# Weight decode in a one-core attention and MLP kernel: a ScalarE byte read for the low word's bits, and a PSUM bank for the scaled word

## The chip, the cores and the metric

The kernel runs on one core of a Trainium2 chip. The metric is device time in microseconds (us). The core's engines are TensorE (PE, its weight loads PEld), VectorE (DVE), ScalarE (ACT), GpSimd (POOL) and SyncE (SP, which issues the DMAs). Each runs its own instructions strictly in the order of its queue.

## The reference, cut to what matters

```
attn = chunked_attention(q, k, v, mem_k, mem_v)     # 4 x 8 heads x 768 x 64, chunks of 32, window 16+32+8 and 8 memory keys
x  = attn as (3072, 512)
h  = x @ w_in                                        # 512 -> 2048
g  = (a0 + a1 h + a2 h^2 + a3 h^3) / (1 + |b0||h| + |b1| h^2 + 1e-6)
x  = g @ w_out                                       # 2048 -> 512
y  = ((x @ w1) * (x @ w2)) @ w3 @ w_out              # 512 -> 1024, gated, 1024 -> 1024 -> 512
```

The second MLP's matrices are called w1, w2 (together w12), w3 and w_out2 in the kernel. The MLP weights arrive as 64-bit floats; the kernel itself turns each word into a 32-bit float and splits that into two fp32r parts, a high one and a remainder. Every matrix product is made of three TensorE products (high x high, high x low, low x high).

## The kernel before

The 3072 tokens are eight blocks of 384. For every block six attention units (`attend`) fill `xr`, then sixteen steps of the first MLP follow: `gemm1` (12 matmuls into a bank of the PSUM ring `h`), the rational function on ScalarE, GpSimd and VectorE, and four steps later `gemm2` (12 matmuls into the banks acc0 to acc3). After 128 such steps the second MLP runs: `gemm3` (two times 12 matmuls into `h`, called `ab` in the trace), a gate, and `gemm4`; w3 and w_out2 are first multiplied with each other (`w3o`), row block by row block.

Weights come in 72 chunks of 128x512 words, each handled by `decode`: 32 for the first block's steps (w_in, w_out), and 40 for the second MLP (16 of w12, 8 of w_out2, 16 of w3), most of which lie within the last sixteen steps of the first MLP and the time after. A chunk takes a slot of the ring `raw` (4 slots, SBUF) and then:

- `load` (L210): a DMA of 512 KB, issued by SP once the slot's last reader is done.
- `scale` (L214, ScalarE): the word's upper half, read as a float, times 2^-112, in place.
- `low` (L218, VectorE): the lower half shifted right by 29, in place.
- two `join`s (L222, VectorE): upper half shifted left by 3 or'ed with those bits, then the sign bit or'ed in. Both inputs and the output lie in SBUF.
- `high_part` (L226, ScalarE) and `low_part` (L229, GpSimd) write the two parts into wA, wB or w3's tiles; then the slot is free.

The order of all work is the result of a planner, `order`: each piece is a `step` with a nominal time `t`, a cost per engine, the steps it comes after and the rings that it takes a buffer of. The planner's list is written out in that order, so every engine's queue is fixed before the run. The PSUM banks are rings too: `h` has three, `att` one (used by the attention units of all blocks but the first for scores, transposes and outputs in turn), acc0 to acc3 one each. `w3o` takes `acc3` and `att` by turns.

Of the kernel before, what the change touches and what calls it, by code (L numbers as in the profile page):

```python
# [26 lines left out]
NF1 = F1 // P  # L27
# [7 lines left out]
SIGN = -2 ** 31  # L35
# [3 lines left out]
def attention_rational_mlp_gated_mlp(  # L39
# [15 lines left out]
    pe, act, dve, pool, sp = nc.tensor, nc.scalar, nc.vector, nc.gpsimd, nc.sync  # L55
# [11 lines left out]
    wB = const.tile([P, NF1, 2, DM], F32R, name="wB")  # L67
# [6 lines left out]
    att = ExitStack()  # L74
# [7 lines left out]
    def bank(tag, name):  # L82
        return ps.tile([P, DM], F32, tag=tag, bufs=rings[tag], name=name)
# [111 lines left out]
    def raw(name):  # L195
        return rawp.tile([P, DM, 2], I32, tag="raw", name=name)

# [3 lines left out]

    def decode(t, src, dst, *ready, take=(), early=(), LOW=None):

        r, d = [], []

        def load():
            r.append(raw("w64"))
            sp.dma_start(out=r[0], in_=src.bitcast(I32).rearrange("p (k t) -> p k t", t=2))  # L210

        def scale():
            hi = r[0][:, :, 1].bitcast(F32)
            act.activation(out=hi, in_=hi, func=AF.Copy, scale=2.0 ** -112)  # L214

        def low():
            lo = r[0][:, :, 0]
            dve.tensor_scalar(out=lo, in0=lo, scalar1=29, scalar2=None, op0=ALU.logical_shift_right)  # L218

        def join(op, n):  # L220
            lo, hi = r[0][:, :, 0], r[0][:, :, 1]
            dve.scalar_tensor_tensor(out=lo, in0=hi, scalar=n, in1=lo, op0=op, op1=ALU.bitwise_or)  # L222

        def high_part():
            d.append(dst() if callable(dst) else dst)
            act.activation(out=d[0][:, 0], in_=r[0][:, :, 0].bitcast(F32), func=AF.Copy)  # L226

        def low_part(eng):
            eng.tensor_tensor(out=d[0][:, 1], in0=r[0][:, :, 0].bitcast(F32), in1=d[0][:, 0].bitcast(F32),  # L229
                              op=ALU.subtract)  # L230

        a = step(t, {"dma": 1.46}, load, *early, take=("raw",))
        b = step(t, {"act": 0.58}, scale, a)
        c = step(t, {"dve": 0.335}, low, a, port=True)
        c = step(t, {"dve": 0.602}, lambda: join(ALU.logical_shift_left, 3), b, c, port=True)
        c = step(t, {"dve": 0.602}, lambda: join(ALU.bitwise_and, SIGN), c, port=True)
        h = step(t + H0, {"act": 0.58}, high_part, c, *ready, take=take)
        l = step(t + H0, LOW or LOWA, low_part, h, frees=[a], port=True)
        a.until.append(h)
        return h, l  # L240

    def mm3(out_, w, wi, x, xi, first, last):
# [112 lines left out]
    def rat_inv(n, i):  # L355
# [3 lines left out]
        else:  # L359
            act.activation(out=h, in_=Q, func=AF.Exp, scale=-1.0)  # L360

# [134 lines left out]
    PAIR7 = two('d', .551, .27); LOWB = two('p', 1.225, .602); GLO7 = two('p', .956, .469); GATE = two('p', .956, .469)  # L496
    LOWA, PAIR, GLO, XLO = two('p', 1.225, .602), two('p', .551, .27), two('p', .956, .469), two('d', 1.764, .87)
    H0 = 1.098
    FIN = {"act": 0.48, "dve": 0.6}

    def start():
# [71 lines left out]

    for u in range(UPB):
        attend(u)
    for t, o, f in chunks:
        (WO if o else WI)[f] = decode(t, *((w_out[f], wB[:, f]) if o else (w_in[f], wA_slot(f))))
    u = UPB
    for n in range(n1):
        ffn1(n)  # L580
# [10 lines left out]
    sec = step(n1 - 16, {"none": 0.0}, second, *VL.values(), v_[NU - 1], tc_[NU - 1])  # L591
# [9 lines left out]
    DW, D3, DV = -2.122, -5.330, -1.521  # L601
    W12, WO2, W3, OP, G3, G4, X2 = {}, {}, {}, {}, {}, {}, {}
    for f in range(NF1):
        W12[f] = decode(tG[f // 2] + f % 2 * 0.4 + DW, w12[f], wA_slot(f), G1[n1 - NF1 + f], early=[G1[n1 - NF1 + max(0, f - 1)]], LOW={"dve": .602} if f < 0 else LOWB)
    for j in range(NF2):
        WO2[j] = decode(tO[0] + DV + 0.3 * j, w_out2[j], wB[:, j], G2[n1 - NF1 + j], early=[G2[n1 - NF1 + j]], LOW=LOWB)

    def x2(blk):
        t = tG[blk * NF2]
# [43 lines left out]
        gates[m] = ffn2_in(m)  # L653
    O = {}
    for i in range(NF2):
        W3[i] = [decode(tO[i] + 0.5 * g + D3, w3T[i, :, g], w3_dst(i, g), sec, take=("w3",), early=[sec] if i < 2 else [O[i - 2]], LOW=LOWB) for g in range(2)]
        t = tO[i]
        tag = ("acc3", "att")[i % 2]
        o = O[i] = step(t, {"pe": 5.61}, lambda i=i: w3o(i), *[x for p in W3[i] for x in p], *[x for p in WO2.values() for x in p],
                 G2[n1 - 1], *([G4[i - 2]] if i > 1 else []), take=(tag,), frees=[p[0] for p in W3[i]])  # L660
# [82 lines left out]
```

## Time and profile before

| | |
|---|---|
| median of 3 runs | 1188.74 us (1188.38 to 1191.08) |
| the profiled execution | 1193.64 us, of which span 1191.8 us |
| busy, share of the span | PE 94%, PEld 87%, DVE 56%, ACT 56%, POOL 40% |
| mean granted TensorE clock | 0.983 |

The whole-span shares hide three stages. In the first 180 us or so the weights of the first MLP are decoded beside the first block and PE has gaps; from there to about 655 us PE is never idle; between 655 and 797 us, where the second MLP's weights are decoded, it has gaps again; then it is busy to the end. Busy shares of a stretch, and what the engines wait for in it, say what limits it.

### The profile page before, as it was taken

The numbers are of one execution on the slowest core, as the hardware profiler recorded it, in microseconds if no ns is written. First come the engines' busy times: TensorE is split into PE (matmuls) and PEld (weight loads), VectorE is DVE, ScalarE is ACT, GpSimd is POOL, SyncE is SP. The second block draws the span as 40 slices with busy tenths as digits, with TensorE's granted clock in tenths as the row PEclk, the third lists the DMA queues.
The fourth block names the chain that finished last, engine by engine and source line by source line (L and its number), as shares of the span: only waits on it lengthen the run. The fifth ranks groups of instructions, "written<-read, shape, count | busy, mean of one in ns | idle before, by whom it ended". The sixth has DMA issues, their size and how long they took to land.

```text
span 1191.8 us, 18531 instructions
## 1 busy us (share of the span) xinstructions
PE 1121.2 (94%) x7104; PEld 1042.2 (87%) x7104; DVE 668.2 (56%) x1249; ACT 667.0 (56%) x1267; POOL 476.4 (40%) x444
## 2 busy tenths in 40 slices
PE   5587699999999999999999799989999999999998
PEld 4476589999999999999999699978889999999997
DVE  6799896667776677676767878855301010110100
ACT  4576687777787777777777866543312222222121
POOL 2466665444444444444444556633211111111111
PEclk9988799999999999999999999989999999999999
DMA  8535322121121121211220232643101101011000
GB/s 241 153 89 167 107 89 63 37 69 37 47 63 36 43 66 44 62 37 43 74 95 1 76 123 84 210 137 107 36 27 54 53 1 53 1 53 54 1 27 27
DMA packets 28028, 83.07 MB, mean 70 GB/s; under 512 B 3746, under 2 KB 3874, under 8 KB 27938
## 3 DMA queue, kind: packets, MB, share of 16 engines
q1 hardware_dynamic: 27648, 81.80, 22.1%
q8 instruction: 56, 0.92, 0.3%
q14 instruction: 32, 0.26, 0.1%
q10 hardware_dynamic: 292, 0.09, 0.0%
HBM read 69.30 MB, written 12.58 MB: 69 GB/s over the span
## 4 chain that ended last, share of the span: by engine, by line
PE 76%; DVE 7%; DMA 5%; ACT 5%; POOL 4%; issue 3%; SPq 0%; POOLq 0%; DVEq 0%; ACTq 0%
PE acc L245 28%; PE ab L245 19%; PE h L245 18%; PE w3o L245 4%; PE sc L262 3%; DVE w L222 2%; DMA w<-in_w_dram 2%; PE xo L308 2%; POOL wA L229 2%; DMA w<-in_w_in_dram 2%; DMA w<-in_w_out_dram 2%; PE at L299 1%; DVE w L218 1%; POOL wB L229 1%; ACT A L334 1%
## 5 line engine op out<-in xcount | busy, mean ns | idle before, releaser
L245 PE MATMUL h<-xr,wA 128*128 128x384 f32 x1536 | 308.7, 351 | 27.9 <-DVE A L372 26.7
L245 PEld LDWEIGHTS h<-xr,wA 128*128 128x128 f32 x1536 | 277.6, 195 | 35.6 <-DVE A L372 30.8
L245 PE MATMUL acc<-gh,wB 128*128 128x384 f32 x1024 | 287.4, 343 | 1.5 <-POOL wB L229 1.5
L245 PE MATMUL ab<-xr,wA 128*128 128x384 f32 x1536 | 280.1, 337 | 5.0 <-DVE W L460 4.5
L245 PEld LDWEIGHTS ab<-xr,wA 128*128 128x128 f32 x1536 | 271.2, 189 | 10.8 <-DVE W L460 5.1
L346 POOL TENSOR_TENSOR W<-W,Q 128x384 f32<-128x384 f32 x128 | 132.9, 1038 | 211.1 <-ACT Q L342 172.6
L460 DVE TENSOR_TENSOR W<-W,ab 128x384 f32<-128x384 f32 x64 | 35.4, 553 | 288.7 <-PE ab L245 287.5
L245 PEld LDWEIGHTS acc<-gh,wB 128*128 128x128 f32 x1024 | 186.2, 188 | 7.4 <-POOL wB L229 2.3
L245 PE MATMUL acc<-gl,wB 128*128 128x384 f32 x512 | 171.7, 335 | 0.0
L469 POOL TENSOR_TENSOR gl<-W,gh 128x384 fp32r<-128x384 f32 x56 | 56.8, 1016 | 280.4 <-ACT gh L464 280.4
L381 POOL TENSOR_TENSOR gl<-A,gh 128x384 fp32r<-128x384 f32 x128 | 136.7, 1069 | 41.1 <-ACT gh L376 33.9
L364 DVE SCALAR_TENSOR_TENSOR A<-A,cf,h 128x384 f32<-128x384 f32 x128 | 78.0, 609 | 102.4 <-ACT h L360 101.8
L222 DVE SCALAR_TENSOR_TENSOR w<-w 128x512 int32<-128x512 int32 x144 | 119.7, 854 | 5.9 <-ACT w L214 5.3
L456 ACT COPY W<-ab 128x384 f32<-128x384 f32 x64 | 30.7, 480 | 142.8 <-PE ab L245 142.8
L334 ACT ACTIVATE A<-h,cf 128x384 f32<-128x384 f32 x128 | 85.5, 668 | 43.0 <-PE h L245 42.3
L358 ACT ACTIVATE Q<-W,one 128x384 f32<-128x384 f32 x128 | 78.9, 616 | 41.0 <-POOL W L346 40.5
L245 PEld LDWEIGHTS acc<-gl,wB 128*128 128x128 f32 x512 | 96.4, 188 | 0.0
L464 ACT CAST gh<-W 128x384 fp32r<-128x384 f32 x56 | 28.7, 512 | 117.2 <-DVE W L460 110.7
L342 ACT ACTIVATE Q<-W,cf 128x384 f32<-128x384 f32 x128 | 90.8, 709 | 4.0
L245 PE MATMUL acc<-wB,gh 128*128 128x512 f32 x294 | 92.2, 394 | 0.0
L351 DVE TENSOR_TENSOR A<-A,h 128x384 f32<-128x384 f32 x128 | 70.1, 548 | 15.9 <-ACT W L334 14.2
L353 DVE SCALAR_TENSOR_TENSOR A<-A,cf,h 128x384 f32<-128x384 f32 x128 | 77.7, 607 | 2.3 <-ACT W L334 0.6
(61 smaller groups left out, 1401.4 us busy)
## 6 DMA issues: line engine op xcount, KB each, us to landing
qk<-in_qkT_dram SPq DMA_DIRECT2D x48, 320.0 KB, 3.9
w<-in_w_out_dram SPq DMA_DIRECT2D x24, 512.0 KB, 4.5
v<-in_vW_dram SPq DMA_DIRECT2D x48, 192.0 KB, 2.4
w<-in_w_in_dram SPq DMA_DIRECT2D x16, 512.0 KB, 4.8
w<-in_w3T_dram SPq DMA_DIRECT2D x16, 512.0 KB, 3.8
w<-in_w_dram SPq DMA_DIRECT2D x16, 512.0 KB, 4.5
x2d<-x2o SPq DMA_DIRECT2D x16, 384.0 KB, 2.7
x<-x2d SPq DMA_DIRECT2D x16, 384.0 KB, 4.1
```

What stands on the lines that cost most here:

```text
L222: dve.scalar_tensor_tensor(out=lo, in0=hi, scalar=n, in1=lo, op0=op, op1=ALU.bitwise_or)
L229: eng.tensor_tensor(out=d[0][:, 1], in0=r[0][:, :, 0].bitcast(F32), in1=d[0][:, 0].bitcast(F32), op=ALU.subtract)
L245: pe.matmul(out_, lhsT=wi(w, a), rhs=xi(x, c), start=first and i == 0, stop=last and i == 2)
L334: act.activation(out=t, in_=hps[n][src], func=func, scale=scale, bias=bias)
L342: act.activation(out=t, in_=hps[n]["W"], func=AF.Identity, scale=cf[:, 5:6], bias=cf[:, 4:5])
L346: pool.tensor_tensor(out=W, in0=W, in1=Q, op=ALU.mult)
L351: dve.tensor_tensor(out=A, in0=A, in1=h, op=ALU.mult)
L353: dve.scalar_tensor_tensor(out=A, in0=A, scalar=cf[:, 1:2], in1=h, op0=ALU.add, op1=ALU.mult)
L358: act.activation(out=Q, in_=W, func=AF.Ln, bias=one)
L364: dve.scalar_tensor_tensor(out=A, in0=A, scalar=cf[:, 0:1], in1=r, op0=ALU.add, op1=ALU.mult)
L381: eng.tensor_tensor(out=gl, in0=hps.pop(n)["A"], in1=gt[n].bitcast(F32), op=ALU.subtract)
L469: eng.tensor_tensor(out=gl, in0=hps.pop(m), in1=gt[m].bitcast(F32), op=ALU.subtract)
```

## The change

`decode` gets two options. With `byte`, the lower half's top three bits are no longer shifted out by VectorE: ScalarE reads the lower half's top byte (every eighth byte of the chunk), multiplies it by 1/32, subtracts 0.484375 and writes the rounded integer in the lower half's place. With `tag`, `scale` writes to a PSUM bank of the ring `tag` instead of in place; the first join reads that bank and the lower half and writes the bank, the second reads the upper half (SBUF) and the bank and writes SBUF. `inps`, the form in which the value stays in PSUM, is used by no chunk, since all low parts are GpSimd's.

In the first MLP all 32 chunks take the byte read, and of each three one is untagged, one takes a bank of `h`, one the bank `att` (11, 11 and 10 chunks). In the second MLP every other chunk takes both options, with bank `att` (20 of 40); the others are as before. `w3o` now takes `acc3` alone. One nominal time (R[1], that of the step |h|) moves from 0.64 to 0.92, and the planner's cost of a join is 0.64 where it reads PSUM. In the listings after the change line numbers are larger: `scale` is L220, the byte read L226, the VectorE shift L228, the joins L233 and L235, `high_part` L243, `low_part` L246.

```diff
-    def decode(t, src, dst, *ready, take=(), early=(), LOW=None):
+    def decode(t, src, dst, *ready, take=(), early=(), LOW=None, tag=None, byte=False):
...
         def scale():
             hi = r[0][:, :, 1].bitcast(F32)
-            act.activation(out=hi, in_=hi, func=AF.Copy, scale=2.0 ** -112)
+            b.append(bank(tag, "wx") if tag else hi)
+            act.activation(out=b[0], in_=hi, func=AF.Copy, scale=2.0 ** -112)
-        def low():
+        def low(eng):
             lo = r[0][:, :, 0]
-            dve.tensor_scalar(out=lo, in0=lo, scalar1=29, scalar2=None, op0=ALU.logical_shift_right)
+            if eng is act:
+                top = r[0].bitcast(U8).rearrange("p k (t b) -> p k t b", b=4)[:, :, 0, 3]
+                act.activation(out=lo, in_=top, func=AF.Copy, scale=1.0 / 32, bias=-0.484375)
+            else:
+                dve.tensor_scalar(out=lo, in0=lo, scalar1=29, scalar2=None, op0=ALU.logical_shift_right)
-        def join(op, n):
-            lo, hi = r[0][:, :, 0], r[0][:, :, 1]
-            dve.scalar_tensor_tensor(out=lo, in0=hi, scalar=n, in1=lo, op0=op, op1=ALU.bitwise_or)
+        def join(i):
+            lo, hi, x = r[0][:, :, 0], r[0][:, :, 1], b[0].bitcast(I32)
+            if i == 0:
+                dve.scalar_tensor_tensor(out=x if tag else lo, in0=x, scalar=3, in1=lo, op0=ALU.logical_shift_left, op1=ALU.bitwise_or)
+            else:
+                dve.scalar_tensor_tensor(out=x if inps else lo, in0=hi, scalar=SIGN, in1=x if tag else lo, op0=ALU.bitwise_and,
+                                         op1=ALU.bitwise_or)
...
-        b = step(t, {"act": 0.58}, scale, a)
-        c = step(t, {"dve": 0.335}, low, a, port=True)
-        c = step(t, {"dve": 0.602}, lambda: join(ALU.logical_shift_left, 3), b, c, port=True)
-        c = step(t, {"dve": 0.602}, lambda: join(ALU.bitwise_and, SIGN), c, port=True)
+        s = step(t, {"act": 0.58}, scale, a, take=(tag,) if tag else ())
+        c = step(t, {"act": 0.58} if byte else {"dve": 0.335}, low, a, port=not byte)
+        J = {"dve": 0.64 if tag else 0.602}
+        c = step(t, J, lambda: join(0), s, c, port=not tag)
+        c = step(t, J, lambda: join(1), c, frees=[a] if inps else [s], port=not tag)
...
-        o = w3os[i] = bank(("acc3", "att")[i % 2], "w3o")
+        o = w3os[i] = bank("acc3", "w3o")
...
+    TAGS, BYTE, LOWS = (None, "h", "att"), (True,), (LOWA,)
+    TAGT, BYTT, LOWT = (None, "att"), (False, True), (LOWA,)
...
-    R = (0.00,0.64,0.28,0.40,0.44,0.36,0.64,0.52,0.83,0.81,1.11,1.39,1.21,1.59)
+    R = (0.00,0.92,0.28,0.40,0.44,0.36,0.64,0.52,0.83,0.81,1.11,1.39,1.21,1.59)
```

Three places in the queues. First VectorE near its start, before the change. The names w_110, w_127, w_152 are three chunks' raw slots; L218 is the shift, L222 a join; e, sc and sm belong to the attention.

```order
L222 SCALAR_TENSOR_TENSOR w_110<-w_110 128x512
L218 TENSOR_SCALAR w_127<-w_127 128x512
L218 TENSOR_SCALAR w_152<-w_152 128x512
L273 TENSOR_REDUCE mx<-sc 128x4
L222 SCALAR_TENSOR_TENSOR w_127<-w_127 128x512
L276 TENSOR_TENSOR e_84<-sc,mx 128x384
L222 SCALAR_TENSOR_TENSOR w_127<-w_127 128x512
```

The same place after the change. The shifts are gone from VectorE, and the tagged chunk w_127 is joined through the bank wx.

```order
L235 SCALAR_TENSOR_TENSOR w_110<-w_110 128x512
L233 SCALAR_TENSOR_TENSOR wx<-wx,w_127 128x512
L293 TENSOR_TENSOR e_84<-sc,mx 128x384
L235 SCALAR_TENSOR_TENSOR w_127<-w_127,wx 128x512
L290 TENSOR_REDUCE mx<-sc 128x4
```

Second, ScalarE after the change, at the tenth and eleventh step of the first MLP. L226 is a byte read; L351, L359, L375, L377 and L393 are the rational function's instructions. The chunk w_656, whose byte read stands first here, is one that takes the bank att.

```order
L226 ACTIVATE w_656<-w_656 128x512
L243 ACTIVATE wA<-w_484 128x512
L297 ACTIVATE e_85<-e_85 128x384
L393 CAST gh<-A 128x384
L375 ACTIVATE Q<-W,one 128x384
L377 ACTIVATE h<-Q 128x384
L351 ACTIVATE A<-h,cf 128x384
L351 ACTIVATE W<-h 128x384
L359 ACTIVATE Q<-W,cf 128x384
L226 ACTIVATE w_696<-w_696 128x512
```

And the place 31 rows later in the same queue at which that chunk's scale, which waits for the bank, stands.

```order
L319 COPY aT<-at 96x512
L226 ACTIVATE w_729<-w_729 128x512
L226 ACTIVATE w_866<-w_866 128x512
L220 ACTIVATE wx<-w_656 128x512
L393 CAST gh<-A 128x384
L334 CAST xr<-xo 128x4x64
```

So the byte reads moved into the queue of the rational function, and a tagged chunk can hold its raw slot from its byte read to a scale that is queued far behind it. Third, PE at the products of w3 and w_out2, before the change (w3o are those products, acc gemm4, ab gemm3).

```order
L245 MATMUL ab<-xr,wA 128x384 x24
L245 MATMUL w3o<-wB,w_8521 128x512 x12
L245 MATMUL w3o<-wB,w_8555 128x512 x12
L245 MATMUL acc<-wB 128x512 x9
L245 MATMUL w3o<-wB,w_8582 128x512 x12
L245 MATMUL w3o<-wB,w_8612 128x512 x12
L245 MATMUL acc<-wB 128x512 x9
```

After the change.

```order
L262 MATMUL w3o<-wB,w_8469 128x512 x12
L262 MATMUL w3o<-wB,w_8474 128x512 x12
L262 MATMUL acc<-wB 128x512 x9
L262 MATMUL ab<-xr,wA 128x384 x12
L262 MATMUL w3o<-wB,w_8544 128x512 x12
L262 MATMUL w3o<-wB,w_8550 128x512 x12
L262 MATMUL acc<-wB 128x512 x9
```

Twelve matmuls of gemm3 now stand between gemm4 and the next w3o, which takes the same bank as the w3o before it; the first w3o stands behind 240 matmuls of gemm3 instead of 312.

## Rows read from the trace of the kernel before

**Rows 1.** Windows: length, then busy us (and count) by engine, granted clock, DMA.

```profile
core 0: us, PE busy (x) PEld busy (x) DVE busy (x) ACT busy (x) POOL busy (x), PEclk, DMA share, GB/s
0.00:42.00 42.00, 21.63 (x216) 16.96 (x216) 30.66 (x61) 18.27 (x35) 15.38 (x16) 1.00 0.72 198
42.00:192.00 150.00, 120.11 (x791) 108.75 (x792) 131.12 (x239) 110.40 (x210) 92.50 (x77) 0.90 0.40 122
655.00:727.00 72.00, 59.82 (x324) 57.27 (x324) 61.33 (x97) 55.88 (x107) 42.75 (x37) 0.98 0.29 96
727.00:797.00 70.00, 65.51 (x359) 64.59 (x358) 50.30 (x73) 38.20 (x71) 43.23 (x33) 0.95 0.49 164
```

**Rows 2.** PE's waits over the whole span: us in total, times, longest.

```profile
PE h L245 <- DVE A L372: 26.7, 14, 4.9
PE xo L308 <- ACT aT L302: 12.0, 7, 3.9
PE at L299 <- POOL e L294: 10.5, 5, 5.1
```

**Rows 3.** VectorE's instruction groups, 0 to 192 us: busy, mean ns, idle before.

```profile
L222 DVE SCALAR_TENSOR_TENSOR w<-w 128x512 int32<-128x512 int32 x64 | 51.4, 828 | 0.3 <-ACT w L214 0.3
L218 DVE TENSOR_SCALAR w<-w 128x512 int32<-128x512 int32 x32 | 26.0, 826 | 6.9 <-DMA w<-in_w_in_dram 5.5 <-DMA w<-in_w_out_dram 1.3
...
L502 DVE MEMSET one<- 128x1 f32 x1 | 0.1, 59 | 0.8 <-PEq L732 0.8
```

**Rows 4.** ScalarE's instruction groups, 0 to 192 us: the first and the last.

```profile
L214 ACT ACTIVATE w<-w 128x512 f32<-128x512 f32 x32 | 21.8, 680 | 15.4 <-DMA w<-in_w_in_dram 9.5 <-DMA w<-in_w_out_dram 5.8
...
L508 ACT ACTIVATE cf<-cf 128x4 f32<-128x4 f32 x1 | 0.2, 189 | 0.0
```

**Rows 5.** Single lines over the span: duration ns min/median/max, first and last start.

```profile
L222 DVE SCALAR_TENSOR_TENSOR w<-w x144: 660/684/1817, 11.4 to 847.8; 128x512 int32<-128x512 int32 x144
L218 DVE TENSOR_SCALAR w<-w x72: 414/428/1552, 9.8 to 846.2; 128x512 int32<-128x512 int32 x72
L214 ACT ACTIVATE w<-w x72: 651/679/708, 9.8 to 845.4; 128x512 f32<-128x512 f32 x72
L368 DVE SCALAR_TENSOR_TENSOR h<-W,one,h x128: 591/615/625, 56.6 to 732.8; 128x384 f32<-128x384 f32 x128
L444 DVE TENSOR_TENSOR spare<-w3o,spare x1: 691/691/691, 802.6 to 802.6; 128x512 fp32r<-128x512 f32 x1
L442 ACT ACTIVATE spare<-w3o x1: 598/598/598, 802.0 to 802.0; 128x512 fp32r<-128x512 f32 x1
```

**Rows 6.** ScalarE's waits, 0 to 192 us.

```profile
ACT wA L226 <- DVE w L222: 17.6, 10, 2.9
ACT w L214 <- DMA w<-in_w_in_dram: 9.5, 8, 3.2
ACT e L280 <- DVE e L276: 8.7, 7, 2.6
ACT w L214 <- DMA w<-in_w_out_dram: 5.8, 6, 2.0
```

**Rows 7.** Timeline of all engines near 780 us: start, duration, idle before.

```profile
778.03 2.41 DVE L222 SCALAR_TENSOR_TENSOR w<-w 128x512 int32<-128x512 int32 x2
...
780.36 0.54 DVE L460 TENSOR_TENSOR W<-W,ab 128x384 f32<-128x384 f32 x1
...
780.96 15.41 PE L245 MATMUL ab<-xr,wA 128*128 128x384 f32 x72 [4.09 <-DVE W L460]
```

**Rows 8.** The chain that ended last, near 810 us: start, duration, what.

```profile
809.66 4.17 PE ab L245 x24
813.84 5.60 PE w3o L245 x24
```

More of the change, by code (lines that the diff above doesn't have):

```diff
@@ L10 @@
 I32 = mybir.dt.int32
+U8 = mybir.dt.uint8
 AF = mybir.ActivationFunctionType
@@ L199, in raw32 @@
         return raw(name).rearrange("p k t -> p (k t)").bitcast(F32)
-    def decode(t, src, dst, *ready, take=(), early=(), LOW=None):
-        r, d = [], []
+    def decode(t, src, dst, *ready, take=(), early=(), LOW=None, tag=None, byte=False):
+        r, d, b = [], [], []
+        LOW = LOW or LOWA
+        inps = tag and "pool" not in LOW
         def load():
@@ new lines, in join, with value @@
+        def join(i):
[5 more added lines that the diff above has]
+                                         op1=ALU.bitwise_or)
+        def value():
+            return b[0] if inps else r[0][:, :, 0].bitcast(F32)
@@ L224, in high_part @@
         def high_part():
             d.append(dst() if callable(dst) else dst)
-            act.activation(out=d[0][:, 0], in_=r[0][:, :, 0].bitcast(F32), func=AF.Copy)
+            act.activation(out=d[0][:, 0], in_=value(), func=AF.Copy)
         def low_part(eng):
-            eng.tensor_tensor(out=d[0][:, 1], in0=r[0][:, :, 0].bitcast(F32), in1=d[0][:, 0].bitcast(F32),
-                              op=ALU.subtract)
+            eng.tensor_tensor(out=d[0][:, 1], in0=value(), in1=d[0][:, 0].bitcast(F32), op=ALU.subtract)
@@ L237, in decode @@
+        J = {"dve": 0.64 if tag else 0.602}
+        c = step(t, J, lambda: join(0), s, c, port=not tag)
+        c = step(t, J, lambda: join(1), c, frees=[a] if inps else [s], port=not tag)
         h = step(t + H0, {"act": 0.58}, high_part, c, *ready, take=take)
-        l = step(t + H0, LOW or LOWA, low_part, h, frees=[a], port=True)
-        a.until.append(h)
+        l = step(t + H0, LOW, low_part, h, frees=[s] if inps else [a], port=not inps)
+        (s if inps else a).until.append(h)
         return h, l
@@ L494, in two @@
         return {g: c for g, c in (("pool", p), ("dve", d)) if g[0] in v}
-    PAIR7 = two('d', .551, .27); LOWB = two('p', 1.225, .602); GLO7 = two('p', .956, .469); GATE = two('p', .956, .469)
-    LOWA, PAIR, GLO, XLO = two('p', 1.225, .602), two('p', .551, .27), two('p', .956, .469), two('d', 1.764, .87)
+    PAIR7 = two('d', .551, .27); LOWB = two('p', 1.225, .64); GLO7 = two('p', .956, .469); GATE = two('p', .956, .469)
+    LOWA, PAIR, GLO, XLO = two('p', 1.225, .64), two('p', .551, .27), two('p', .956, .469), two('d', 1.764, .87)
     H0 = 1.098
+    TAGS, BYTE, LOWS = (None, "h", "att"), (True,), (LOWA,)
+    TAGT, BYTT, LOWT = (None, "att"), (False, True), (LOWA,)
     FIN = {"act": 0.48, "dve": 0.6}
@@ L575, in attention_rational_mlp_gated_mlp @@
         attend(u)
-    for t, o, f in chunks:
-        (WO if o else WI)[f] = decode(t, *((w_out[f], wB[:, f]) if o else (w_in[f], wA_slot(f))))
+    for k, (t, o, f) in enumerate(chunks):
+        (WO if o else WI)[f] = decode(t, *((w_out[f], wB[:, f]) if o else (w_in[f], wA_slot(f))), tag=TAGS[k % len(TAGS)], byte=BYTE[k % len(BYTE)], LOW=LOWS[k % len(LOWS)])
     u = UPB
@@ L603, in attention_rational_mlp_gated_mlp @@
     for f in range(NF1):
-        W12[f] = decode(tG[f // 2] + f % 2 * 0.4 + DW, w12[f], wA_slot(f), G1[n1 - NF1 + f], early=[G1[n1 - NF1 + max(0, f - 1)]], LOW={"dve": .602} if f < 0 else LOWB)
+        W12[f] = decode(tG[f // 2] + f % 2 * 0.4 + DW, w12[f], wA_slot(f), G1[n1 - NF1 + f], early=[G1[n1 - NF1 + max(0, f - 1)]], LOW=LOWT[f % len(LOWT)], tag=TAGT[f % len(TAGT)], byte=BYTT[f % len(BYTT)])
     for j in range(NF2):
-        WO2[j] = decode(tO[0] + DV + 0.3 * j, w_out2[j], wB[:, j], G2[n1 - NF1 + j], early=[G2[n1 - NF1 + j]], LOW=LOWB)
+        WO2[j] = decode(tO[0] + DV + 0.3 * j, w_out2[j], wB[:, j], G2[n1 - NF1 + j], early=[G2[n1 - NF1 + j]], LOW=LOWT[j % len(LOWT)], tag=TAGT[j % len(TAGT)], byte=BYTT[j % len(BYTT)])
     def x2(blk):
@@ L655, in attention_rational_mlp_gated_mlp @@
     for i in range(NF2):
-        W3[i] = [decode(tO[i] + 0.5 * g + D3, w3T[i, :, g], w3_dst(i, g), sec, take=("w3",), early=[sec] if i < 2 else [O[i - 2]], LOW=LOWB) for g in range(2)]
+        W3[i] = [decode(tO[i] + 0.5 * g + D3, w3T[i, :, g], w3_dst(i, g), sec, take=("w3",), early=[sec] if i < 2 else [O[i - 2]], LOW=LOWT[g % len(LOWT)], tag=TAGT[g % len(TAGT)], byte=BYTT[g % len(BYTT)]) for g in range(2)]
         t = tO[i]
-        tag = ("acc3", "att")[i % 2]
         o = O[i] = step(t, {"pe": 5.61}, lambda i=i: w3o(i), *[x for p in W3[i] for x in p], *[x for p in WO2.values() for x in p],
-                 G2[n1 - 1], *([G4[i - 2]] if i > 1 else []), take=(tag,), frees=[p[0] for p in W3[i]])
+                 G2[n1 - 1], *([G4[i - 2]] if i > 1 else []), take=("acc3",), frees=[p[0] for p in W3[i]])
         d = []
```

## Prediction

> **What bounds the kernel now.** I read the windows first, because the whole-span shares say nothing about stages. PE is the engine whose gaps cost time, and it has them in two places: 50.3 us in the first 192 us (192 less 21.63 and 120.11), and 12.2 + 4.5 us between 655 and 797 us [rows 1]. In between it is full, and nothing that decode does can shorten that.
>
> The list of PE's waits then says whom it waits for: VectorE's last instruction of the rational function, which frees a bank of h (26.7 us), and the attention's ScalarE and GpSimd steps (12.0 and 10.5) [rows 2]. These are ends of chains, so the next question is which engine on them is full. From 42 to 192 us VectorE is busy for 131.1 of 150 us, ScalarE for 110.4, GpSimd for 92.5 [rows 1]: VectorE is the fullest and everything on the chains queues behind it. Its groups show on what: 64 joins of 828 ns and 32 shifts of 826 ns, 77.4 us of durations for decode alone [rows 3]. The fastest shift takes 414 ns and the fastest join 660 [rows 5]. The excess appears only on these two kinds of lines; an instruction of the same VectorE with an input in PSUM (L368) stays within 591 and 625 ns over 128 executions [rows 5].
>
> **Durations and occupancy.** Durations of neighbours overlap, so a sum of them is not time. ScalarE's 16 groups in the first 192 us sum to 142.8 us (the first and the last stand in [rows 4]), and its busy time is 18.27 + 110.40 = 128.7 [rows 1], with 245 instructions: each occupies 0.058 us less than it lasts. VectorE's 15 groups sum to 178.0 (first and last in [rows 3]), its busy time is 161.8, with 300 instructions [rows 1]: 0.054 less. I cost every added or removed instruction by its duration less that.
>
> **First stage, removed from VectorE.** 32 shifts at 0.826 less 0.054 are 24.7 us. 42 of the 64 joins (21 tagged chunks) now have one input in SBUF and one in PSUM. Such a join is not in the trace. The bounds are 0.660 (the fastest join) and 0.828 (no change); I take 0.691, that of L444, which reads 512 columns from PSUM and as many from SBUF [rows 5]. That gives 42 x 0.137 = 5.8 us, with 0 and 7.1 as bounds. VectorE falls from 161.8 to 131.3.
>
> **Added to ScalarE.** 32 byte reads. The trace has no read of single bytes. The nearest row is scale itself, which steps through the same slot with the same stride: 680 ns, 651 to 708 [rows 4, 5]; the lower bound is L442, 512 columns without a stride, 598 ns [rows 5]. At 0.680 less 0.058 this is 19.9 us, with 17.3 and 20.8 as bounds. A scale that writes PSUM costs the same or, at 598, 21 x 0.082 = 1.7 us less; I take the same. ScalarE rises from 128.7 to 148.6.
>
> The Trainium skill, ScalarE: Activation LUTs, section "What ACT_TABLE_LOAD costs", has a lower price: 186 ns plus 0.833 per element, and 93 ns of overlap between neighbours, so an estimate by that page is 520 ns of occupancy per byte read, 16.6 us in all. By it the whole sum below would end at 14.5 us of gain instead of 11.2. The row does not agree (680 ns, and 58 of overlap), and I go by the row.
>
> **What it does to the stage.** The bound moves from VectorE with 161.8 to ScalarE with 148.6, 13.2 us lower. VectorE was idle for 30.2 of the 192 us, 192 less 161.8. If ScalarE idled as long, the same work would end at 178.8. I add 4 us: of the two engines that a load feeds, ScalarE waits longer for it, 15.3 us (9.5 + 5.8) [rows 6] against the 6.9 before VectorE's shift [rows 3], and about half of the difference of 8.4 stays when ScalarE is the full engine. So the stage ends 9.2 us earlier. The part of GpSimd in it only falls (92.5 of 150 us), since its work stays and fewer VectorE instructions read two SBUF inputs. The granted clock of 0.90 between 42 and 192 [rows 1] is PE at 1.2 instead of 2.4 GHz after its gaps; I count nothing for it.
>
> **Second stage, 655 to 727 us.** Between the 112th and the 128th step the queues hold 7 byte reads more on ScalarE and 9 shifts instead of 14 on VectorE. ScalarE goes from 55.9 to 60.2 (7 x 0.62), VectorE from 61.3 to some 57 (5 x 0.77; tagged joins take a little more). The full engine changes from 61.3 to 60.2 of 72: I count 0, with 4 us lost as bound if ScalarE's chains are the longer ones, 2 us won as the other.
>
> **727 to 797 us.** PE's 4.5 us of idle time here are almost one wait of 4.09 us: the gate's multiplication L460 stands behind joins of 1.2 us each in VectorE's queue, and gemm3 waits for the bank that it frees [rows 7]. The clock of 0.95 over these 70 us adds 3.5 us [rows 1]. With half of the shifts gone this queue has slack (50.3 of 70 busy before). But the first w3o stands 72 matmuls earlier, so decode has less time. I take 3 us of gain, between 0 and 8.
>
> **w3o with one bank.** Each w3o now waits until L442 and L444 have emptied the bank: 0.598 + 0.691 = 1.29 us [rows 5]. In front of it stand 12 matmuls of gemm3, half of 4.17, so 2.1 us [rows 8]: covered, with 0.8 to spare. If a decode instruction is ahead in both queues (0.68 and 0.69), it is short by 0.6; seven times that is 4 us. I take 1 us. The w3o themselves (5.60 us) do not change.
>
> **Sum.** -9.2 - 0 - 3 + 1 = -11.2 us, against the profiled execution's 1193.6: 1182.4. The median of the runs shown is 1188.7, 0.4% below that execution, so I predict 1178 (1177.5).
>
> **Rivals.** (1) Slower: the raw slots and the bank att. A chunk with that bank keeps its slot from its byte read to a scale that stands up to 31 instructions later in ScalarE's queue, since the attention uses the same bank; with one of four slots held, loads are issued later, and the scale and the byte read stand in front of the rational function. Its price is read from the waits that ScalarE has for loads today, 14 in 15.3 us, 1.1 each [rows 6]: one more such wait for each of the 21 tagged chunks is 23 us, so 148.6 + 30.2 + 23 = 201.8, 9.8 us later than 192, and with 2 us from the second stage 1197. It decides from 0.63 us per tagged chunk (13.2/21). For it: ScalarE is the first to touch a load and is now the full engine. Against it: the waits for joins (17.6) and for the attention's subtraction (8.7) [rows 6] get shorter.
>
> (2) No change: six of the rational function's instructions per step are ScalarE's, each waits for another engine, and its idle time rises to some 43 us, so that the stage ends where it did; with 2 us from the second stage 1187.
>
> (3) More gain: the 17.6 us that ScalarE waits for joins [rows 6] halve, since VectorE is no longer full. Idle 30.2 less 8 is 22: the stage ends at 170.8, 21.2 us earlier, with the second stage 23 us, 1166.
>
> **How the numbers follow.** This kernel's measurement can tell 0.3% from no change, 3.6 us. The forecast case has 0.53 (its own range is -5 to -18 us, 1171 to 1184, from 27 to 40 us of ScalarE idle time), rival 3 0.14, rival 2 0.16, rival 1 0.17. Faster is the forecast and rival 3, 0.67; same 0.16; slower 0.17. The range holds the first three and the edge of the last: 1164 to 1192.
>
> **What the new profile would show.** Right: in the first 180 us VectorE some 130 us busy, ScalarE near 149, PE without gaps some 10 us earlier than before; byte reads of 650 to 710 ns; tagged joins near 690 with a narrow spread; the 4 us wait near 780 gone; between w3o no PE waits above 1 us. Wrong: byte reads far from 680; ScalarE waiting for loads or for the bank of att for more than 40 us in all; PE waiting at w3o for L444; VectorE still the fullest engine.

## The result and the profile after

The changed kernel takes 1169.62 us (median of 4 runs, 1168.86 to 1172.52), the kernel before 1189.25 (4 runs, 1188.38 to 1191.08). The ratio is 0.9837 with a 95% interval of 0.9817 to 0.9858, so the change saves 19.6 us. 1178 was forecast: a gain, but little more than half of the real one.

The windows of the kernel after, with the columns of [rows 1]:

```profile
core 0: us, PE busy (x) PEld busy (x) DVE busy (x) ACT busy (x) POOL busy (x), PEclk, DMA share, GB/s
0.00:42.00 42.00, 21.83 (x216) 17.07 (x216) 25.49 (x57) 24.63 (x48) 13.70 (x16) 1.00 0.83 228
42.00:192.00 150.00, 128.67 (x873) 117.74 (x874) 117.56 (x226) 129.21 (x248) 89.11 (x82) 0.94 0.38 114
655.00:727.00 72.00, 66.33 (x360) 64.86 (x361) 62.85 (x100) 62.61 (x118) 47.22 (x41) 0.95 0.36 110
727.00:797.00 70.00, 68.66 (x352) 62.49 (x352) 41.14 (x54) 36.35 (x66) 34.45 (x27) 1.00 0.50 161
...
0.00:180.00 180.00, 138.49 (x998) 123.29 (x998) 133.86 (x262) 144.09 (x276) 97.89 (x93) 0.95 0.50 146
```

The full engine of the first stage has changed, as forecast: between 42 and 192 us VectorE falls from 131.1 to 117.6 and ScalarE rises from 110.4 to 129.2. PE is busy for 8.6 us longer in the same 150 us and gets through 873 matmuls instead of 791.

Windows at equal times hold different work in the two kernels, so a sum can only be compared up to the same point of the work. The last row ends at such a point: PE is never idle from there to the marker described below, and in the kernel before the same holds from 192 us on. First the row of the kernel before up to its point, then the stretch from there to the marker, before and after:

```profile
0.00:192.00 192.00, 141.74 (x1007) 125.72 (x1008) 161.78 (x299) 128.67 (x244) 107.89 (x93) 0.92 0.47 138
192.00:342.60 150.60, 150.60 (x1120) 142.48 (x1119) 105.49 (x220) 114.23 (x221) 69.28 (x73) 1.00 0.16 45
179.95:330.58 150.63, 150.63 (x1130) 142.41 (x1130) 107.52 (x225) 114.18 (x221) 69.31 (x73) 1.00 0.17 47
```

**Where the time went.** Queue SP stores the finished 384 columns of a block of the first MLP, which gives a marker that lies at the same work in all kernels: its third store is at 342.63 us before and here after.

```profile
250.65 1.14 SPq L418 DMA_DIRECT2D x2d<-x2o  x2
330.58 0.82 SPq L418 DMA_DIRECT2D x2d<-x2o  x2
```

So 12.05 us are won in the first stage (the second store, 262.14 before, gives 11.5), and nothing more until the second MLP's decode: the store that stands at 584.16 before is at 572.09, 12.07 earlier. From there to the start of the last gemm1 of the first MLP (720.93 before, 705.57 after, 15.36 earlier) another 3.3 us are won, and from there to the end 5.7, since the span is 21.1 shorter (1191.8 to 1170.7). The two profiled executions differ by 1.5 us more than the medians do. These are the stretches with the same work behind the first stage, two before and two after:

```profile
655.00:720.93 65.93, 54.22 (x294) 51.98 (x293) 55.26 (x90) 50.12 (x96) 38.57 (x33) 0.97 0.29 96
720.93:1191.80 470.87, 462.29 (x2376) 426.17 (x2376) 125.56 (x186) 134.87 (x251) 117.88 (x101) 0.99 0.17 58
643.00:705.57 62.57, 54.78 (x293) 52.99 (x292) 52.78 (x88) 55.28 (x105) 41.24 (x36) 0.95 0.37 118
705.57:1170.70 465.13, 459.73 (x2377) 423.61 (x2376) 117.99 (x167) 139.57 (x261) 113.02 (x99) 1.00 0.17 56
```

So PE's idle time falls by 8.7 us in the first stage (192.00 less 141.74 is 50.3; 180.00 less 138.49 is 41.5), by 3.9 in the second and by 3.2 behind it. The rest is PE's busy time for the same matmuls: 3.3 us less in the first stage, where the granted clock goes from 0.92 to 0.95, 0.6 more in the second (0.97 to 0.95) and 2.6 less behind it (0.99 to 1.00).

The groups of decode in the first 180 us, ScalarE's first, with the columns of [rows 4]:

```profile
L226 ACT ACTIVATE w<-w 128x512 int32<-128x512 uint8 x32 | 21.2, 666 | 2.6 <-DMA w<-in_w_in_dram 1.8 <-DMA w<-in_w_out_dram 0.8
...
L220 ACT ACTIVATE wx<-w 128x512 f32<-128x512 f32 x21 | 13.3, 634 | 10.7 <-DMA w<-in_w_in_dram 8.6 <-DMA w<-in_w_out_dram 1.8
...
L220 ACT ACTIVATE w<-w 128x512 f32<-128x512 f32 x11 | 7.4, 675 | 8.2 <-DMA w<-in_w_in_dram 5.1 <-DMA w<-in_w_out_dram 3.0
```

and VectorE's, with the columns of [rows 3]:

```profile
L233 DVE SCALAR_TENSOR_TENSOR wx<-wx,w 128x512 int32<-128x512 int32 x21 | 14.6, 694 | 8.5 <-ACT w L226 8.2 <-ACT wx L220 0.2
L235 DVE SCALAR_TENSOR_TENSOR w<-w,wx 128x512 int32<-128x512 int32 x21 | 14.3, 682 | 0.6
...
L235 DVE SCALAR_TENSOR_TENSOR w<-w 128x512 int32<-128x512 int32 x11 | 9.0, 821 | 0.1
L233 DVE SCALAR_TENSOR_TENSOR w<-w 128x512 int32<-128x512 int32 x11 | 8.4, 764 | 3.0 <-ACT w L226 2.9
```

A byte read lasts 666 ns (680 forecast). The joins that read PSUM last 694 and 682 (691 forecast), the others 764 and 821. Over the whole span the tagged joins hardly vary, and the untagged ones reach 1.8 us (lines L233 and L235: shortest, median, longest):

```profile
L233 DVE SCALAR_TENSOR_TENSOR wx<-wx,w x41: 680/692/700, 14.6 to 820.3; 128x512 int32<-128x512 int32 x41
L235 DVE SCALAR_TENSOR_TENSOR w<-w,wx x41: 656/689/692, 15.6 to 821.1; 128x512 int32<-128x512 int32 x41
L235 DVE SCALAR_TENSOR_TENSOR w<-w x31: 660/695/1804, 13.9 to 819.7; 128x512 int32<-128x512 int32 x31
```

PE's waits over the span answer to [rows 2]; the third is new:

```profile
PE h L262 <- DVE A L389: 9.1, 6, 2.3
PE xo L325 <- ACT aT L319: 8.7, 5, 4.9
...
PE at L316 <- DVE w L235: 7.5, 2, 5.5
```

The wait for the bank of h has fallen from 26.7 to 9.1 us. The new wait is the attention's, for the bank att that a decode chunk holds.

### The profile page after: what moved, and what is told of

Same layout as the page of the kernel before. It is cut to its first block, busy times and chain, and to the rows that moved or that the text cites. A ratio compares the mean times of both kernels' runs of the same rounds, so it can differ in the third digit from the quotient of the medians.

```text
span 1170.7 us, 18521 instructions
## 1 busy us (share of the span) xinstructions
PE 1116.0 (95%) x7104; PEld 1038.1 (89%) x7104; DVE 632.0 (54%) x1197; ACT 692.3 (59%) x1319; POOL 462.9 (40%) x444
## 4 chain that ended last, share of the span: by engine, by line
PE 78%; ACT 6%; DMA 6%; DVE 5%; issue 2%; POOL 2%; SPq 0%; POOLq 0%; ACTq 0%; DVEq 0%
PE acc L262 29%; PE ab L262 19%; PE h L262 19%; PE w3o L262 4%; PE sc L279 3%; DMA w<-in_w_out_dram 3%; DMA w<-in_w_in_dram 2%; PE xo L325 2%; PE at L316 1%; DVE w L235 1%; DMA qk<-in_qkT_dram 1%; ACT Q L359 1%; POOL wA L246 1%; ACT wA L243 1%; ACT Q L375 1%
## 5 line engine op out<-in xcount | busy, mean ns | idle before, releaser
L262 PE MATMUL h<-xr,wA 128*128 128x384 f32 x1536 | 302.4, 346 | 11.9 <-DVE A L389 9.1
L262 PE MATMUL acc<-gh,wB 128*128 128x384 f32 x1024 | 291.4, 347 | 5.8 <-ACT wB L243 3.0
L262 PEld LDWEIGHTS h<-xr,wA 128*128 128x128 f32 x1536 | 272.7, 192 | 18.4 <-DVE A L389 11.2
L363 POOL TENSOR_TENSOR W<-W,Q 128x384 f32<-128x384 f32 x128 | 131.3, 1026 | 214.3 <-ACT Q L359 177.7
L262 PEld LDWEIGHTS acc<-gh,wB 128*128 128x128 f32 x1024 | 188.7, 191 | 12.2 <-POOL wB L246 4.5
L398 POOL TENSOR_TENSOR gl<-A,gh 128x384 fp32r<-128x384 f32 x128 | 131.7, 1029 | 44.8 <-ACT gh L393 37.6
L351 ACT ACTIVATE A<-h,cf 128x384 f32<-128x384 f32 x128 | 85.4, 667 | 37.0 <-PE h L262 36.5
L375 ACT ACTIVATE Q<-W,one 128x384 f32<-128x384 f32 x128 | 79.0, 617 | 38.2 <-POOL W L363 37.5
L359 ACT ACTIVATE Q<-W,cf 128x384 f32<-128x384 f32 x128 | 90.8, 709 | 4.2
L385 DVE SCALAR_TENSOR_TENSOR h<-W,one,h 128x384 f32<-128x384 f32 x128 | 78.6, 614 | 0.2
```

Of the source, the lines that this page charges most:

```text
L262: pe.matmul(out_, lhsT=wi(w, a), rhs=xi(x, c), start=first and i == 0, stop=last and i == 2)
L351: act.activation(out=t, in_=hps[n][src], func=func, scale=scale, bias=bias)
L363: pool.tensor_tensor(out=W, in0=W, in1=Q, op=ALU.mult)
L375: act.activation(out=Q, in_=W, func=AF.Ln, bias=one)
L385: dve.scalar_tensor_tensor(out=r, in0=W, scalar=one, in1=r, op0=ALU.add, op1=ALU.mult)
L398: eng.tensor_tensor(out=gl, in0=hps.pop(n)["A"], in1=gt[n].bitcast(F32), op=ALU.subtract)
```

## The experiments

Every kernel is given as a ratio to the kernel before, timed on the same chip; that kernel's median was 1190.7 to 1192.6 us there, so 0.001 is 1.2 us. "Marker" is the third store, 342.63 before and 330.58 after the change. Where an edit alters what the planner is told, the order is planned anew; "the change's order" and "the order of before" mean that the queues were kept. "The same point of the work" is the place where 192 us lies in the kernel before, 150.6 us ahead of the marker; PE is never idle between the two in any kernel for which it is given here. A marker is read from one execution, and executions of one kernel spread by 2.6 to 6.9 us over the whole run, so one or two us between markers say nothing.

**The parts by themselves.** First, the byte reads without any bank: no chunk is tagged, and w3o has its two banks again.

```
-    TAGS, BYTE, LOWS = (None, "h", "att"), (True,), (LOWA,)
-    TAGT, BYTT, LOWT = (None, "att"), (False, True), (LOWA,)
+    TAGS, BYTE, LOWS = (None,), (True,), (LOWA,)
+    TAGT, BYTT, LOWT = (None,), (False, True), (LOWA,)
```

> The byte read alone: all chunks joined in SBUF, w3o on two banks as before the change, the queues planned anew. Occupancy theory (the gain is VectorE's shifts moved to ScalarE): within 4 us of the full change, 1166 to 1174. Port theory (the gain is that tagged joins and GpSimd no longer hold each other up): most of the gain goes, 1178 or more.

Measured: 0.9851 (0.9833 to 0.9869), marker 329.1. Newly planned, the byte reads alone bring what the whole change brings. VectorE is relieved far less than the shifts were worth: up to the same point of the work it is busy for 151.5 us instead of 161.8, since its joins now last 972 and 1080 ns, while ScalarE does 14.7 us more (143.4 instead of 128.7). The window of the byte-only kernel up to that point

```profile
0.00:178.46 178.46, 137.97 (x1007) 123.52 (x1008) 151.45 (x266) 143.41 (x275) 104.92 (x93) 0.94 0.52 149
```

and its joins, with the columns of [rows 3]:

```profile
L235 DVE SCALAR_TENSOR_TENSOR w<-w 128x512 int32<-128x512 int32 x32 | 34.3, 1080 | 0.1
L233 DVE SCALAR_TENSOR_TENSOR w<-w 128x512 int32<-128x512 int32 x32 | 30.8, 972 | 4.0 <-ACT w L226 3.3 <-issue 0.7
```

Then the banks without the byte reads:

```
-    TAGS, BYTE, LOWS = (None, "h", "att"), (True,), (LOWA,)
-    TAGT, BYTT, LOWT = (None, "att"), (False, True), (LOWA,)
+    TAGS, BYTE, LOWS = (None, "h", "att"), (False,), (LOWA,)
+    TAGT, BYTT, LOWT = (None, "att"), (False,), (LOWA,)
```

> The PSUM bank alone: same tags as the change, all shifts on VectorE, queues planned anew. Occupancy theory: VectorE in the first stage falls by 42 x 0.137 = 5.8 us only and stays the full engine, so a gain of about 6 us in all, 1180 to 1187. Port theory: at least 12 us of gain, 1177 or less.

Measured: 0.9958 (0.9942 to 0.9974), marker 342.4. In the first stage they bring nothing (342.63 before); what there is, 5 us, comes later. VectorE is relieved by 9.3 us up to the same point of the work, and the stage does not end earlier for it:

```profile
0.00:191.79 191.79, 138.64 (x1008) 124.03 (x1009) 152.47 (x297) 128.86 (x243) 100.06 (x92) 0.94 0.48 138
```

Then the first MLP's part alone, with the second MLP's decode untagged and on VectorE, and w3o in two banks:

```
-    TAGT, BYTT, LOWT = (None, "att"), (False, True), (LOWA,)
+    TAGT, BYTT, LOWT = (None,), (False,), (LOWA,)
-        o = w3os[i] = bank("acc3", "w3o")
+        o = w3os[i] = bank(("acc3", "att")[i % 2], "w3o")
```

> The change in the 32 chunks of the first MLP alone; the 40 chunks of the second MLP and w3o's two banks as before the change. If the two stages' gains are separate, as the traces say (12 us up to the second block, 9 us behind it): 1177, 1174 to 1180. If the first stage alone makes the gain: 1170.

Measured: 0.9904 (0.9876 to 0.9932), 11.4 us, with the marker at 331.6. The two MLPs are in the main separate terms: the first stage's gain stays, and most of what the change won behind it is gone. From the store at 573.14 to the last gemm1 at 708.21 this kernel takes 1.7 us less than the one before (135.07 against 136.77), where the change takes 3.3 less, and from there to its end at 1179.4 nothing less (471.2 against 470.9). Its windows there, which lie 11 us further in the work than those of [rows 1]:

```profile
655.00:727.00 72.00, 65.36 (x346) 63.06 (x345) 62.76 (x102) 54.92 (x104) 44.05 (x37) 0.93 0.29 92
727.00:797.00 70.00, 65.43 (x340) 62.21 (x339) 44.80 (x61) 32.98 (x60) 37.70 (x30) 0.95 0.48 157
```

**The change's order, with one cost put back.** The scaled word of a tagged chunk stays in SBUF, in the queues of the change, and no bank is taken. Only where the joins read differs:

```
+        plan, tag = tag, None
-        s = step(t, {"act": 0.58}, scale, a, take=(tag,) if tag else ())
+        s = step(t, {"act": 0.58}, scale, a, take=(plan,) if plan else ())
-        J = {"dve": 0.64 if tag else 0.602}
+        J = {"dve": 0.64 if plan else 0.602}
```

> The changed kernel with every queue in the same order, but the tagged chunks' scaled word stays in place in SBUF and no bank is taken. Occupancy theory: tagged joins go from 0.69 to about 0.83 us, some 6 us in the first stage on an engine that is no longer the full one, and PE's 7.5 us of waits for the bank att vanish: -2 to +4 us against the change, 1167 to 1174. Port theory: +8 us or more, 1178 or more.

Measured: 0.9958 (0.994 to 0.9975), marker 341.05: in this order the PSUM joins are worth 0.0121, 14.4 us. This is what the port theory expected, and not the theory by which only the fullest engine's sum counts. The joins are longer than the 0.83 us that the expectation took: up to 180 us the first lasts 911 ns and the second 1128 on average. Line L237 is the second one (shortest, median, longest):

```profile
L237 DVE SCALAR_TENSOR_TENSOR w<-w x72: 664/1091/1773, 13.6 to 838.3; 128x512 int32<-128x512 int32 x72
```

ScalarE's waits for loads and joins from 0 to 192 us:

```profile
ACT w L222 <- DMA w<-in_w_in_dram: 15.1, 11, 3.2
...
ACT wA L245 <- DVE w L237: 3.6, 3, 2.0
```

With both inputs in SBUF the median is 1091 ns, against 689 for the second join of the change's tagged chunks. What the longer joins hold up is not shown in full: ScalarE's waits for loads are not longer than after the change (19.3 us in all against 21.1), those for joins are 4.7 instead of 1.1. Up to the same point of the work VectorE does 16.5 us more than after the change (150.4 against 133.9), and of the 10.5 us by which that point comes later, 4.0 are idle time of PE and 6.5 its busy time for the same matmuls (144.9 against 138.4):

```profile
0.00:190.42 190.42, 144.90 (x998) 128.41 (x998) 150.40 (x262) 144.79 (x276) 106.29 (x93) 0.93 0.49 138
```

Then the shift back on VectorE, again in the change's order (`low` only tests `eng`; the step keeps its place):

```
-            if eng is act:
+            if eng is None:
```

> The changed kernel with the same order of pieces, but the 52 byte reads of ScalarE are shifts on VectorE again, at the same places. Occupancy theory: VectorE has 25 us more in the first stage and is the full engine again, +8 to +15 us against the change, 1178 to 1185. Port theory: +4 us at most, under 1174.

Measured: 0.9866 (0.9848 to 0.9885), marker 329.0, before the change's own 330.58. The move off VectorE is worth 0.0029 here, 3.5 us, and the two intervals overlap. VectorE is the fullest engine again, with 151.1 us up to the same point of the work where it had 133.9, and the stage ends no later for it:

```profile
0.00:178.35 178.35, 136.12 (x997) 120.59 (x997) 151.07 (x294) 128.46 (x244) 101.40 (x93) 0.96 0.51 147
```

Its instructions are those of the banks-only kernel, which has 0.9958. Only their order differs: 0.0092, 11 us. Up to the same point of the work the two engines do as much in both (VectorE 151.1 and 152.5, ScalarE 128.5 and 128.9), and the point comes 13.4 us earlier in the one.

Of the two theories, that the fullest engine's sum sets the stage (occupancy) and that joins and GpSimd hold each other up (port), neither covers these runs: the byte-only and the banks-only kernel came out as the first expects, the two kernels in the change's order as the second does. For the next kernels a third theory is set against the first: that the order of the queues counts.

**The order of before, with the shift moved.** All 52 shifts that the change moves become byte reads on ScalarE, issued where the shift stood in the program, untagged:

```
-            dve.tensor_scalar(out=lo, in0=lo, scalar1=29, scalar2=None, op0=ALU.logical_shift_right)
+            if byte:
+                top = r[0].bitcast(mybir.dt.uint8).rearrange("p k (t b) -> p k t b", b=4)[:, :, 0, 3]
+                act.activation(out=lo, in_=top, func=AF.Copy, scale=1.0 / 32, bias=-0.484375)
```

> The kernel before, every queue in its order, all joins in SBUF, but the change's 52 shifts are done as byte reads on ScalarE at the places of the plan. Occupancy theory: VectorE falls by some 25 us in the first stage, ScalarE becomes the full engine, 8 to 13 us faster than before, ratio 0.989 to 0.993. Order theory: 0 to 4 us, ratio 0.997 or more.

Measured: 1.0011 (0.9998 to 1.0024), marker 344.1. The move brings nothing. These are the same instructions as in the byte-only kernel (0.9851): the order alone is worth 0.016, 19 us. The window up to the same point of the work:

```profile
0.00:193.45 193.45, 142.93 (x1007) 126.73 (x1008) 146.69 (x267) 144.75 (x276) 104.21 (x93) 0.91 0.47 137
```

and VectorE's longest wait up to 180 us:

```profile
DVE w L226 <- ACT w L220: 14.9, 9, 6.1
```

VectorE is busy for 15.1 us less than before (161.78 less 146.69), and waits 14.9 us for the byte reads, up to 6.1 us at a time: its joins keep their places, but what they need now stands behind other work in ScalarE's queue. In the byte-only kernel the same wait is 3.3 us. It is 11.1 us in the changed kernel, though (8.2 and 2.9 in its groups above), so this wait by itself does not set the stage's end.

**The shift left out.** In the change's order the byte reads are not issued, and the first join takes the word's upper half in their place; then the same in the order of before.

```
-                act.activation(out=lo, in_=top, func=AF.Copy, scale=1.0 / 32, bias=-0.484375)
-                dve.scalar_tensor_tensor(out=x if tag else lo, in0=x, scalar=3, in1=lo, op0=ALU.logical_shift_left, op1=ALU.bitwise_or)
+                dve.scalar_tensor_tensor(out=x if tag else lo, in0=x, scalar=3, in1=hi if byte else lo, op0=ALU.logical_shift_left, op1=ALU.bitwise_or)
```

> The changed kernel in its own order, with the 52 byte reads left out altogether, so neither ScalarE nor VectorE takes out those bits (the first join reads the upper half in their place; the output is not the reference's). Occupancy theory (the fullest engine sets the first stage, and after the change that is ScalarE): ScalarE has 20 us less there, VectorE 134 us is the next limit, 8 us or more faster than the change, a ratio to before of 0.977 or less. Order theory (what counts is the order of the queues and the chains through them): within 3 us of the change, 0.981 to 0.986.

> The kernel before in its order, with the same 52 shifts left out and nothing in their place (the first join reads the upper half twice; the output is not the reference's). Occupancy theory: VectorE loses 25 us in the first stage and ScalarE gains none, 20 us or more faster, ratio 0.983 or less. Order theory: at most 6 us, ratio 0.995 or more.

Measured: 0.9754 (0.9729 to 0.9779), marker 322.5, and 0.9871 (0.9848 to 0.9893), marker 333.0. The first came out as the occupancy theory expected and against the order theory, the second lies between the two. So the byte reads still cost 0.0083, 9.9 us, where the change has them, and the shifts cost 15.4 us in the order of before. In the change's order without any shift ScalarE's busy time up to the same point of the work is down from 144.0 to 127.4 us, 0.52 for each of 32 byte reads, and the point comes 8.1 us earlier:

```profile
0.00:171.83 171.83, 134.35 (x998) 119.46 (x998) 132.99 (x262) 127.41 (x244) 98.39 (x93) 0.97 0.53 153
```

**Variants.** The bank att left to the attention in the first MLP; a byte read for two of three chunks only; one number of the planner's table; and banks in the second MLP alone. The queues of all four are planned anew, so each has an order of its own beside its edit:

```
+    TAGS, BYTE, LOWS = (None, "h"), (True,), (LOWA,)

+    TAGS, BYTE, LOWS = (None, "h", "att"), (False, True, True), (LOWA,)

-    R = (0.00,0.92,0.28,0.40,0.44,0.36,0.64,0.52,0.83,0.81,1.11,1.39,1.21,1.59)
+    R = (0.00,0.64,0.28,0.40,0.44,0.36,0.64,0.52,0.83,0.81,1.11,1.39,1.21,1.59)

+    TAGS, BYTE, LOWS = (None,), (True,), (LOWA,)
```

> The change with the bank att left out for the first MLP's chunks (untagged and h by turns), queues planned anew. If PE's 7.5 us of waits for that bank are on the path: 4 to 7 us faster than the change, 1163 to 1166. If ScalarE sets the end of the stage and these waits lie beside it: within 2 us, 1168 to 1172.

Measured: 0.9837 (0.9814 to 0.9861), marker 331.8. The same as the change: PE's 7.5 us of waits for the bank att cost nothing that shows. The attention's PE instructions wait here for GpSimd instead, 7.8 us up to 192 us where it was 1.1.

> The change, but in the first MLP the untagged chunks' shifts (11 of 32) stay on VectorE. ScalarE has 11 x 0.61 = 6.7 us less, VectorE some 8 us more in the first stage, so both come to about 137 to 142 of 180. If ScalarE is now the bound of that stage: 2 to 6 us faster, 1164 to 1168. If the chain through both is: no change or up to 3 us slower.

Measured: 0.9873 (0.9846 to 0.99), marker 335.1. Not better, though the two engines are then almost equal up to 180 us (VectorE 139.9, ScalarE 135.9): 4.5 us later in the first stage than the change. This is not idle time of PE, which has 42.1 us of it up to the same point of the work, after the change 41.5. Its busy time for the same matmuls is longer (142.4 against 138.4 us), with a granted clock of 0.91 instead of 0.95:

```profile
0.00:184.46 184.46, 142.37 (x1008) 127.66 (x1009) 143.32 (x276) 139.57 (x264) 98.14 (x92) 0.91 0.50 144
```

> The change with the nominal time of the step |h| back at 0.64, queues planned anew. If that time does nothing by itself: within 2 us, 1168 to 1172. If it carries part of the gain: 3 us or more slower, 1173 or more.

Measured: 0.9841 (0.9814 to 0.9868), marker 331.7: no difference.

> The change with the PSUM banks in the second MLP's chunks alone; the first MLP's chunks take the byte read and are joined in SBUF, queues planned anew. The traces of the change and of the byte read alone give this sum: second block at 248.6 instead of 250.7 us, the rest as in the change: 1 to 3 us faster than the change, ratio 0.981 to 0.984. If the banks are worth something in the first stage: 0.986 or more.

Measured: 0.9827 (0.9803 to 0.985), marker 328.5. This is the lowest ratio of those that do all the work, but its interval covers the change's. No version is shown to beat the change. The run suggests that the first MLP's banks are not needed where the order is planned without them.

## Why the prediction was right or wrong

**Direction and range held.** The time fell and lies in the range, at 1169.6; it is outside the forecast's own range (1171 to 1184), between that and rival 3 (1166). All three terms of the sum were too small, and the first came near its size by luck, on a reason that the runs do not bear out.

**The durations held, the occupancy of a byte read did not.** Byte read 666 ns (0.680 taken), tagged joins 694 and 682 (0.691), scale into PSUM 634 (0.680 taken, 0.598 as bound). But leaving the 32 byte reads out takes 16.6 us off ScalarE up to the same point of the work (144.0 less 127.4), 0.52 us each where the prediction took 0.622: the mean overlap of 0.058 was too small for them. The lower price that the prediction set aside, its estimate by the Trainium skill, ScalarE: Activation LUTs, section "What ACT_TABLE_LOAD costs", was 520 ns of occupancy. The runs agree with that price, and with it the sum would have been 14.5 us; they do not agree with the duration behind it, 613 ns by the same estimate and 666 here.

One reading of the prediction goes too far, without harm to its sum: long durations are not found on decode's two lines alone. Over the span of the kernel before L416 lasts between 944 and 1776 ns and L288 between 151 and 937.

**The first stage, -9.2 forecast, -12.05 measured.** ScalarE was to work for 148.6 us and to idle for 34.2 (30.2 + 4). Up to 180 us, the same point of the work, it worked for 144.1 and idled for 35.9: the idle time was right to 2 us, and the work 4.5 smaller; the byte reads explain 3.3 of that (19.9 less 16.6) and the scales into PSUM 1.0 (21 x 0.046). VectorE has 133.9 (131.3 forecast). Seen from PE the 12.05 us are 8.7 of idle time and 3.3 of busy time at a higher granted clock, a term that the prediction counted at nothing. Whether the clock follows the gaps or has a share in them, no run separates.

**The step that failed** is the one before that: "the bound moves from VectorE with 161.8 to ScalarE with 148.6, 13.2 us lower", with the order of the queues left out of account. The fullest engine's sum does not set this stage's end. In the four kernels that follow that sum, VectorE's, lies between 150.4 and 152.5 us up to the same point of the work, and the point comes at 178.35 (VectorE's shift in the change's order), 178.46 (byte reads alone), 190.42 (no banks in the change's order) and 191.79 us (banks alone). With the shift on ScalarE in the order of before VectorE has 146.7 and ScalarE 144.8, and the point comes at 193.45, later than in the kernel before with 161.8. Two pairs of kernels hold the same instructions in two orders each, byte reads (0.9851 and 1.0011) and banks with VectorE's shifts (0.9866 and 0.9958), and the order accounts for 19 us in the one and 11 in the other. In an order that is kept, the move itself was worth between nothing and 3.5 us. I took the new order as something that follows the work; in both pairs it counts for more than the move.

The work itself is not free: leaving the shifts out saves 9.9 us in the one order and 15.4 in the other. After the change VectorE works for 133.9 and ScalarE for 144.1 us of the stage's 180, and VectorE waits for ScalarE's byte reads. An argument that fits, and no more than that, is that removing work helps, while shifting it between them helps only with an order in which the other engine has it done in time.

**The PSUM joins** were counted with 5.8 us of VectorE's time. Their worth depends on the order as well: 14.4 us in the order planned with them, none that shows in the first stage of an order planned without (0.9851 and 0.9827 against 0.9837, all intervals overlapping). The Trainium skill, SBUF — State Buffer, section "Who interferes with whom", says that a VectorE instruction with two SBUF inputs contends with a GpSimd instruction that reads SBUF, and one with a single SBUF input does not. The trace agrees: joins with two SBUF inputs reach 1.8 us and those with a PSUM input, 82 in all, never exceed 700 ns.

**655 to 727 us, 0 forecast, -3.3 measured.** I compared the full engines' sums again (61.3 and 60.2 of 72). In the stretch with the same work, up to the last gemm1, VectorE falls from 55.3 to 52.8 us and ScalarE rises from 50.1 to 55.3, so the fullest engine's sum stays, as forecast, and PE's idle time still falls from 11.7 to 7.8 us, while the clock takes 0.6 back. The bound of 2 us of gain was too tight, on the same reason as in the first stage.

**727 to 797 us, -2 forecast with w3o, -5.7 measured.** The wait of 4.09 us is gone, and PE's waits after 600 us are these, none of them at a w3o:

```profile
PE h L262 <- DVE A L389: 7.8, 5, 2.3
PE ab L262 <- ACT W L473: 1.6, 2, 1.2
```

So the 1 us for the single bank was not spent. From the last gemm1 to the end PE's idle time fell by 3.2 us (8.6 to 5.4), and its busy time for the same matmuls by 2.6, with the granted clock up from 0.95 to 1.00 in the window of 727 to 797 us. I had named both and counted 3 us in all. The mechanism was right, the term mis-sized.

**The rivals.** Rival 1's place exists (the attention's waits for the bank att, 7.5 us; ScalarE's waits for weight loads up from 15.3 to 21.1), but leaving the bank out, in an order planned for that, changes nothing that shows, so its price is far from 23 us. Rival 2, no change, is what the same move does in the order of before. Rival 3's cause came about more than fully, ScalarE's wait for joins is 0.5 us where it was 17.6 (wA's high parts), but its idle time did not fall to 22 us: of the 35.9 us that it is, 21.1 are waits for loads.

**Open.** What in the planner's account makes the new order the better one: the cost of the byte read on ScalarE, the flag that keeps joins off a shared port, or chance. The plan that counts the shift on VectorE gives a worse order for VectorE's shifts than the plan that counts it on ScalarE, so its account does not rank orders well. The instructions of the kernel before were not run in the change's order, so how much of the gain an order alone would give there is not known. An estimate: if in that order the prices of the banks (0.0121) and of the move (0.0029) added up, the ratio without both would be 0.9987, no gain. The order would then pay only together with the instructions that it was planned for, and the 11 and 19 us are no share of the change's 19.6.

## What to carry to other kernels

Where instructions stand in hand-planned queues, moving one to another engine and planning anew are two changes: run each alone before the gain is put down to the move, above all when two engines are both busy for most of a stage and feed each other. An engine's busy sum says how long a stage must last at least if nothing else changes, not when it ends; with 150 to 152 us on the fullest engine the stage ended at 178 us in two kernels here and at 190 and 192 in two others. Such sums are compared up to the same point of the work and not up to the same time, at which the faster kernel has done more. And a window that shows a wait and a lowered clock side by side holds two terms, which can both come back.

## What the runs showed of the hardware

A read of single bytes with a stride of eight lasted as long as a read of floats with that stride (666 and 675 ns for 512 columns). A scale that writes PSUM instead of the strided slot was shorter: 632 against 672 ns as medians over the span:

```profile
L220 ACT ACTIVATE wx<-w x41: 609/632/662, 12.8 to 817.9; 128x512 f32<-128x512 f32 x41
L220 ACT ACTIVATE w<-w x31: 648/672/721, 9.8 to 817.4; 128x512 f32<-128x512 f32 x31
```

A byte read added less to ScalarE's busy time than it lasted: 0.52 us each in the change's order, 0.50 in the order of before (144.75 less 128.67 for 32), for durations of 0.666 and 0.664.

The joins with two SBUF inputs were longer in the kernels without banks: 1080 and 1128 ns on average for the second join in the byte-only kernel (group L235, 0 to 180 us) and in the one that keeps the change's order (L237), 828 for both joins before, with GpSimd about as busy (105.6, 99.6 and 101.2 us of 180). The kernel with the one growth is as fast as the change (0.9851), the one with the other is not (0.9958).
